# Softmax weights of batches 3 to 7: division in place by GpSimd, halves by one copy and one subtraction

## The chip, the cores and the metric

One core of a Trainium2 chip runs the whole program. The metric is the device time of one execution in microseconds; three runs of the kernel before took 893.05, 891.38 and 894.42 us, a median of 893.05 us. The engines are TensorE (PE, matmuls; its weight loads are listed as PEld), VectorE (DVE), ScalarE (ACT), GpSimd (POOL) and SyncE (SP, whose queue issues the DMAs). Each has its own queue and runs it in order.

## The reference

Windowed attention with a linear bias, then a two-layer MLP with an exact GELU, all in float32:

```python
# q, k, v: (8, 8, 576, 64); w_in: (512, 2048); w_out: (2048, 512)
scores = scale * np.matmul(q, k.transpose(0, 1, 3, 2))
mask = (rel >= 0) & (rel < 128)
scores = np.where(mask, scores + bias[None], -1000000000.0)
scores = scores - np.max(scores, axis=-1, keepdims=True)
attn = np.exp(scores)
attn = attn / (np.sum(attn, axis=-1, keepdims=True) + 1e-09)
x = np.matmul(attn, v)           # then 4608 tokens of 512 values
h = x @ w_in
out = (0.5 * h * (1.0 + erf(h / sqrt(2)))) @ w_out
```

## The kernel before

The 4608 tokens are nine tiles of 512; a batch has 576 tokens, so batch b fills tile b and the first part of tile b+1. While tile t goes through the MLP, batch b = t+1 goes through attention. Float32 accuracy comes from two float16 halves: a value is scaled, its high half is the rounded value, its low half the rest, and a product is three matmuls (high by high, high by low, low by high).

**Attention of one batch** is done in four units, each a pair of heads. A unit has nine groups of 128 rows by 192 keys, in two parts: five groups and four. Its steps: the scores on PE go to five PSUM banks (`scores`, L620); DVE scales them, adds the bias and puts them into the float32 tile `s` (`biased`, L646, five instructions, which is what frees the banks; GpSimd fills masked corners); DVE takes each part's maximum (L729); ScalarE takes the exponentials in place, group by group, with their sums `z` (L733); DVE inverts the sums (L736, L737). The high half of exponential times `z` is written to `e_main`: group by group by ScalarE in batches 1 to 3 (L740), by GpSimd in batches 4 to 7 (L742). The low half is one DVE instruction for each group (`low_part`, L305, called in `low_weights`). Then one DMA for each part transposes `e_main` into the unit's tile `et` (L750). There is one `e_main`, so a part's halves can be written only when the transpose of the same part of the unit before has read it; there are two tiles `s`, taken in turn. PE multiplies `et` by the values for two units at once (`weigh_two`, L846), and the result, again as two halves, is the MLP's input.

**The MLP of a tile**: tiles 2 and 3 go through h = x w_in in 16 blocks (L914) and a GELU each; tiles 4, 5 and 6 go through a form with seven products instead of eight (`Middle`, L1285); the second layer is four blocks of 16 steps (`second`, L961), of which each quarter is 12 matmuls of 512 columns. Tiles 7 and 8 follow with a form of their own.

**The order** is written by hand. `ORDER` (tiles 0 and 1) and `LATER` (tiles 2 to 6) are tables of names, and each name takes one step of a generator; the steps are recorded in that order, so the tables set each engine's queue. In `LATER` the first digit is the tile t, the attention steps being of batch t+1: S0 to S3 are the scores of the four units, B the bias steps, M and N the softmax and low halves (unit, part), Y0 and Y1 the two attention products of units 0 and 1 and of units 2 and 3, X what leaves them, Q and V the loads of the next batch's q, k and v, H and g or the digits 1 to 7 the first layer, o0 to o3 the quarters of the second layer, v and q the statistics and halves of the next batch's values, q and k, K the weights' sums that are stored for the later tiles. `LATER_BANKS` says which of eight PSUM banks each new tile of scores or products takes.

Of the kernel before, what the change touches and what calls it, by code (L numbers as in the profile page):

```python
# [104 lines left out]
2M01 2N01 2M00 2H9 2N00 K K 2H9 2M10 2H10 K 2H10 2N01 2H10 K 2N00 2g9 2N01 2H10 2B2 K 2H11 2g7 2B2 K 2H11 2B2 2g10
2H11 2g8 2B2 2M10 2g9 2N00 2H11 2B2 2g10 2B2 2H12 2g9 2B2 2H12 K 2g11 2B2 2H12 2g10 2B2 2H12 2M20 2H13 K K 2H13 2g12
2H13 2g11 2M10 2H13 2g12 2g11 2H14 K 2g12 2H14 2g13 2M21 2H14 K 2H14 K 2H15 2g14 2g13 2H15 2M10 2g14 2g13 2H15 K 2g14
2H15 K 2o0 2M10 2g15 2M10 2M10 2M10 4gs 2o0 2g15 2M10 2N10 2M10 2g15 2M10 2M10 2N10 2M11 2N10 2N10 2o0 2N10 4gs 2N10
2M11 2M11 2M11 K K 2o0 2M20 K 2M20 2M20 2M11 2M20 2M11 K 2M11 2o1 2M11 2k0 K 2M11 2N11 2M11 2k0 K 2M20 2N11 2M21 K
2N11 2M21 2N11 2Q 2o1 K 2M21 2M21 2M20 2M21 2M20 2M21 2S3 2M20 2N11 2M20 2N20 2M20 2N20 2M20 2o1 2B3 2M20 2N20 2B3 2q  # L110
2B3 2N20 2B3 2B3 2N20 2o1 2Q 2B3 2M30 2B3 2B3 2M30 2M21 2Y0 2B3 2M31 2k1 2M21 2k1 2N21 2M21 2N21 2M21 2M30 2N21 2N21
2M30 2o2 2N20 2M30 2M30 2M31 2M30 2M30 2M31 2M31 2o2 2M31 2N21 2X0 2M31 2M31 2q 2X0 2X0 2o2 2M30 2q 2q 2q 2M30 2q 2N30
2M31 2N30 2M30 2N31 2M31 2N30 2M30 2o2 2M31 2N31 2M30 2N30 2M31 2N31 2X0 2N30 2N31 2N30 2X0 2o3 2X0 2X0 2q 2k2 2X0 2X0
2X0 2q 2q 2X0 2N31 2q 2X0 2o3 2q 2q 2q 2q 2q 2q 2q 2q 2q 2k2 2o3 2q 2q 2Y1 2q K K 2o3 2X1 3U 2X1 K 2X1 K 3H0 K 2X1 3H0
# [1540 lines left out]
```

## Time and profile before

| | us |
|---|---|
| median of three runs | 893.05 |
| the profiled execution | 900.88 |
| its span, first to last instruction | 898.9 |
| PE busy | 856.0 (95%) |
| DVE busy | 733.5 (82%) |
| ACT busy | 612.2 (68%) |
| GpSimd busy | 268.4 (30%) |

The profiled execution took 7.83 us more than the median run, and 1.98 us of it lie outside its span. PE's mean granted clock is 0.988 of full speed. PE is busy for nearly the whole span, but its share is a mean: where it stands still for a few microseconds, it waits for another engine or a DMA, and that place is found in the timeline and not in the share. The attention products of batches 3 to 7 and the tiles 2 to 6 lie between 255.7 and 744.9 us of the span.

### The profile page before, as it was taken

To read this page: it belongs to the slowest core of one execution; us is meant where nothing else is said; L and a number is where in the kernel's file an instruction comes from. 1 tells how busy PE (TensorE), PEld (TensorE's weight loads), DVE (VectorE), ACT (ScalarE), POOL (GpSimd) and SP (SyncE) were. 2 spreads that over 40 slices of the span, in tenths; PEclk is the share of its full clock that TensorE was granted. 3 is DMA by queue.
4 is the path that set the end of the run, shared out by engine and by line. 5 is a ranking of instruction groups with operands and counts; after the bars stand their busy time and mean duration, and the time that the engine had idled before them with its cause. 6 is when DMAs were issued, how large, how long until landed. Compare 5 with 4: busy or idle time off the path is not lost. (4 is left out here: it accounts for less than half of the span.)

```text
span 898.9 us, 21140 instructions
## 1 busy us (share of the span) xinstructions
PE 856.0 (95%) x8580; PEld 523.0 (58%) x8580; DVE 733.5 (82%) x1434; ACT 612.2 (68%) x1236; POOL 268.4 (30%) x445
## 2 busy tenths in 40 slices
PE   6999999999999979899899999999899999999998
PEld 4654444544554445445468645875487544588887
DVE  6999899999779956699967997799887989962871
ACT  7999779895778976494639573874568437642850
POOL 1010000222054802957515446344535420000000
PEclk9999999999999989999989999999999999999999
DMA  9665745562540394326742765276642350031201
GB/s 316 250 202 192 256 115 118 143 164 68 128 118 20 83 243 103 118 53 164 172 165 66 204 127 171 94 212 92 159 151 54 78 118 12 1 106 36 95 1 48
DMA packets 178066, 112.78 MB, mean 125 GB/s; under 512 B 134064, under 2 KB 156720, under 8 KB 175792
## 3 DMA queue, kind: packets, MB, share of 16 engines
q1 hardware_dynamic: 177968, 111.43, 44.7%
q8 instruction: 67, 1.10, 0.5%
q14 instruction: 31, 0.25, 0.1%
HBM read 63.31 MB, written 13.63 MB: 86 GB/s over the span
## 5 line engine op out<-in xcount | busy, mean ns | idle before, releaser
L914 PE MATMUL h<-x,wi 128*128 128x512 f16 x960 | 212.5, 379 | 2.6 <-DVE s L646 1.6
L961 PE MATMUL o<-wo,g 128*128 128x512 f16 x864 | 194.4, 381 | 0.4 <-DVE g L305 0.4
L961 PEld LDWEIGHTS <-g 128*128 128x128 f16 x1152 | 111.0, 98 | 135.5 <-issue 3.2
L914 PEld LDWEIGHTS <-wi 128*128 128x128 f16 x960 | 92.7, 98 | 116.7 <-issue 5.4
L733 ACT ACTIVATE s<-s,nmax 128x192 f32<-128x192 f32 x252 | 111.3, 443 | 57.1 <-DVE nmax L729 56.8
L305 DVE SCALAR_TENSOR_TENSOR e_main<-s,z,e_main 128x192 f16<-128x192 f32 x252 | 114.5, 495 | 21.3 <-ACT e_main L740 11.5
L742 POOL TENSOR_SCALAR e_main<-s,z 128x192 f16<-128x192 f32 x144 | 72.3, 520 | 50.5 <-DVE z L737 28.0
L652 POOL MEMSET s<- 64x128 f32 (+1 forms) x112 | 19.3, 173 | 177.4 <-DVE s L646 153.3
L646 DVE SCALAR_TENSOR_TENSOR s<-sc,cs,bias_h 128x384 f32<-128x384 f32 x112 | 66.9, 606 | 2.6 <-PE sc L620 2.3
L961 PE MATMUL o<-wo_first,g 128*128 128x512 f16 x288 | 66.1, 380 | 1.3 <-DVE e_main L305 1.2
L620 PE MATMUL sc<-kbuf,qbuf 64*64 64x192 f16 (+3 forms) x1656 | 50.4, 252 | 12.8 <-ACT qbuf L521 4.4
L1285 PEld LDWEIGHTS <-t 128*128 128x128 f16 x576 | 56.4, 98 | 7.7 <-issue 1.2
L729 DVE TENSOR_REDUCE nmax<-s 128x5 f32<-128x960 f32 (+1 forms) x56 | 58.1, 1043 | 2.7 <-POOL s L652 2.5
L958 PE MATMUL o<-zo,g 128*128 128x512 f32 x128 | 58.6, 610 | 0.0
L939 POOL TENSOR_SCALAR g<-g,sg 128x512 f16<-128x512 f32 x48 | 41.5, 871 | 55.7 <-ACT g L935 28.4
L740 ACT ACTIVATE e_main<-s,z 128x192 f16<-128x192 f32 x108 | 41.1, 443 | 11.8 <-DMA et<-e_main 8.0
L846 PE MATMUL av<-et,vbuf 64*64 64x64 f16 (+1 forms) x1920 | 32.6, 202 | 17.4 <-DMA et<-e_main 11.6
L733 ACT ACTIVATION_READ_ACCUMULATOR s<-s,nmax 128x1 f32 x252 | 47.2, 187 | 0.0
L305 DVE SCALAR_TENSOR_TENSOR g<-g,sg,g 128x512 f16<-128x512 f32 x48 | 43.3, 921 | 3.9 <-POOL g L939 3.8
L1285 PEld LDWEIGHTS <-wi 128*128 128x128 f16 x432 | 41.9, 98 | 6.4 <-DVE x L305 0.7
L935 ACT ACTIVATE g<-h,gs 128x512 f32<-128x512 f32 x48 | 31.6, 685 | 18.4 <-DVE g L305 12.0
L846 PEld LDWEIGHTS <-vbuf 64*64 64x64 f16 (+1 forms) x1920 | 30.1, 117 | 22.4 <-issue 21.7
(275 smaller groups left out, 1604.2 us busy)
## 6 DMA issues: line engine op xcount, KB each, us to landing
t<-stored SPq DMA_DIRECT2D x12, 1024.0 KB, 5.0
v<-vp SPq DMA_DIRECT2D x32, 320.0 KB, 4.9
out<-ob SPq DMA_DIRECT2D x34, 256.0 KB, 2.2
raw<-w_in SPq DMA_DIRECT2D x8, 1024.0 KB, 10.4
raw<-w_out SPq DMA_DIRECT2D x8, 1024.0 KB, 8.0
q<-qp SPq DMA_DIRECT2D x7, 1152.0 KB, 6.0
k<-kp SPq DMA_DIRECT2D x7, 1152.0 KB, 8.3
stored<-sums SPq DMA_DIRECT2D x8, 512.0 KB, 2.8
```

Of the source, the lines that this page charges most:

```text
L305: return nc.vector.scalar_tensor_tensor(out=dst, in0=src, scalar=scale, in1=high, op0=ALU.mult, op1=ALU.subtract)
L620: done = nc.tensor.matmul(ps[bank][o, n, gap:W], a, m[:, gap:W], start=(i == 0 and (n == 0 or b > 0)), stop=(i == len(terms) - 1 and b > 0 ...
L646: yield nc.vector.scalar_tensor_tensor(out=s[:, bank[0] : bank[0] + k, :], in0=ps[bank][:, 0:k, 0:W], scalar=cs, in1=bias.broadcast_to([P, ...
L729: yield nc.vector.tensor_reduce(out=nmax[:, r], in_=s[:, r], axis=AX.X, op=ALU.max, negate=True)
L733: yield nc.scalar.activation(s[:, i, :], s[:, i, :], AF.Exp, bias=nmax[:, i : i + 1], accum_out=z[:, i : i + 1])
L742: yield nc.gpsimd.tensor_scalar(e[:, i, 0, c], s[:, i], z[:, i : i + 1], 1.0, op0=ALU.mult, op1=ALU.mult)
L846: done = nc.tensor.matmul(o, a, m, start=key not in started, stop=left[key] == 0, skip_group_check=True)
L914: done = nc.tensor.matmul(ph, wi[n][:, a, cc, k * P : (k + 1) * P], x[:, cc, b, :], start=(i == 0), stop=(i == 3 * NCC - 1),)
L939: yield nc.gpsimd.tensor_scalar(g[:, r, 0], g32, gsg[t, n], 1.0, op0=ALU.mult, op1=ALU.mult)
L958: done = nc.tensor.matmul(o, g[:, r, c], zo[n][:, n % 2, k * DM : (k + 1) * DM], start=(fc == first), stop=(fc == last))
L961: done = nc.tensor.matmul(o, g[:, r, a, c], wo[n][:, b, k, :], start=(fc == first and i == 0), stop=(fc == last and i == 2),)
L1285: done = nc.tensor.matmul(ps[:, k * HT : (k + 1) * HT], w(a, i)[:, k * P : (k + 1) * P], m(b, i), start=first and n == 0, stop=True, skip_ ...
```

## The change

A table `HALVES` gives each batch a way to make its halves. Batches 0 to 2 keep theirs (batch 0 has none). In batches 3 to 7 GpSimd multiplies the exponentials by `z` in place, so `s` holds the finished weights in float32; one ScalarE copy for each part then writes the high halves, and one DVE subtraction for each part the low halves. The way "g" of the new code is the old way of batches 4 to 7, and no batch uses it. `LATER`, `LATER_BANKS` and the last entries of `LATER_ROOMS` (which output buffer is taken) are made anew; `ORDER` stays. The lines of `LATER` shown are those around the scores S2 and S3 of batch 5.

```diff
+HALVES = "aaawwwww"
...
 LATER = """
...
-4M10 4M11 4M11 4M11 4M10 4M11 4v 4M10 4v 4v 4v 4M10 4v 4M11 4v 4M11 4S2 4M10 4k0 4M11 4N10 4k0 4M10 4o1 4N11 4M11 4B2
-4M10 4N10 4N11 4M11 4N10 4M10 4N11 4M11 4o1 4N10 4B2 4N11 4N10 4N11 4B2 4v 4B2 4B2 4B2 4o1 4N10 4M20 4B2 4B2 4M20 4v
-4M20 4B2 4v 4M21 4M20 4S3 4M20 4v 4v 4M20 4v 4v 4o1 4v 4B3 4M21 4M21 4M20 4v 4B3 4B3 4M21 4M20 4v 4B3 4M21 4B3 4M20
...
+4M11 4M10 4o0 4M10 4v 4M10 4M11 4M11 4M11 4M11 4S2 4M10 4M11 4M10 4M11 4v 4M10 4v 4v 4v 4o0 4v 4B2 4M10 4M10 4v 4v 4B2
+4B2 4M10 4v 4M10 4v 4v 4B2 4B2 4M10 4M11 4B2 4M11 4S3 4k0 4M11 4M11 4N10 4B2 4M11 4o1 4q 4B2 4N10 4N11 4B2 4M20 4o1 4q
...
@@ -736,17 +733,23 @@
         for i in range(r.start, r.stop):
-            if st.b < 4:
+            if HALVES[st.b] == "a":
                 yield nc.scalar.activation(e[:, i, 0, c], s[:, i], AF.Copy, scale=z[:, i : i + 1])
                 continue
-            yield nc.gpsimd.tensor_scalar(e[:, i, 0, c], s[:, i], z[:, i : i + 1], 1.0, op0=ALU.mult, op1=ALU.mult)
+            to = e[:, i, 0, c] if HALVES[st.b] == "g" else s[:, i]
+            yield nc.gpsimd.tensor_scalar(to, s[:, i], z[:, i : i + 1], 1.0, op0=ALU.mult, op1=ALU.mult)
+        if HALVES[st.b] == "w":
+            yield nc.scalar.copy(e[:, r, 0, c], s[:, r])
 
     def low_weights(st, part):
 
         r, c, banks = RANGES[part]
         e = e_main
-        for i in range(r.start, r.stop):
-            yield low_part(e[:, i, 1, c], st.s[:, i], st.z[:, i : i + 1], e[:, i, 0, c])
+        if HALVES[st.b] == "w":
+            yield nc.vector.tensor_tensor(out=e[:, r, 1, c], in0=st.s[:, r], in1=e[:, r, 0, c], op=ALU.subtract)
+        else:
+            for i in range(r.start, r.stop):
+                yield low_part(e[:, i, 1, c], st.s[:, i], st.z[:, i : i + 1], e[:, i, 0, c])
```

SP's queue in tile 2, batch 3, of the kernel before: `et3_1` is the transposed tile of unit 1, `q32_4` and `k32_4` are the loads for batch 4, `stored` the stores of the weights' sums.

```order
L750 DMA_TRANSPOSE et3_1_3857<-e_main_95 128x20x128
L1069 DMA stored1_104<-sums1_0_3738 128x2048
L975 DMA out_0<-ob2_0_3903 128x512
L527 DMA q32_4_3918<-qp 128x4x576
L1069 DMA stored1_104<-sums1_1_3865 128x2048
L750 DMA_TRANSPOSE et3_1_3857<-e_main_95 128x16x128
L527 DMA k32_4_4043<-kp 128x4x576
L975 DMA out_0<-ob2_1_4251 128x512
L750 DMA_TRANSPOSE et3_2_4276<-e_main_95 128x20x128
L750 DMA_TRANSPOSE et3_2_4276<-e_main_95 128x16x128
L750 DMA_TRANSPOSE et3_3_4355<-e_main_95 128x20x128
L750 DMA_TRANSPOSE et3_3_4355<-e_main_95 128x16x128
```

The same place of SP's queue in the changed kernel.

```order
L753 DMA_TRANSPOSE et3_1_3840<-e_main_95 128x20x128
L1072 DMA stored1_104<-sums1_0_3689 128x2048
L753 DMA_TRANSPOSE et3_1_3840<-e_main_95 128x16x128
L524 DMA q32_4_3992<-qp 128x4x576
L978 DMA out_0<-ob2_0_3904 128x512
L1072 DMA stored1_104<-sums1_1_3845 128x2048
L753 DMA_TRANSPOSE et3_2_4265<-e_main_95 128x20x128
L753 DMA_TRANSPOSE et3_2_4265<-e_main_95 128x16x128
L524 DMA k32_4_4300<-kp 128x4x576
L753 DMA_TRANSPOSE et3_3_4321<-e_main_95 128x20x128
L753 DMA_TRANSPOSE et3_3_4321<-e_main_95 128x16x128
```

The second transpose of unit 1 moved ahead of the load of q, and the load of k moved from ahead of unit 2's transposes to between those of units 2 and 3.

DVE's queue in batch 5 of the kernel before, from the first bias step of unit 2 (`s5_2`) on; the rows of `e_main` are the low halves of unit 1.

```order
L646 SCALAR_TENSOR_TENSOR s5_2_6901<-sc5_2_0_6820,cs5_5789,bias_h_64 128x384
L305 SCALAR_TENSOR_TENSOR e_main_95<-s5_1_6735,z5_1_6766,e_main_95 128x192 x7
L646 SCALAR_TENSOR_TENSOR s5_2_6901<-sc5_2_2_6821,cs5_5789,bias_h_64 128x384
L280 TENSOR_REDUCE top_6930<-turned_6817 32x1
L646 SCALAR_TENSOR_TENSOR s5_2_6901<-sc5_2_4_6822,cs5_5789,bias_p_65 128x192
```

The same place in the changed kernel, to the last bias step of unit 2.

```order
L643 SCALAR_TENSOR_TENSOR s5_2_6832<-sc5_2_4_6750,cs5_5808,bias_p_65 128x192
L643 SCALAR_TENSOR_TENSOR s5_2_6832<-sc5_2_5_6751,cs5_5808,bias_h_64 128x384
L977 TENSOR_SCALAR ob4_0_6914<-o4_0_6681,so4_4729 128x512
L749 TENSOR_TENSOR e_main_95<-s5_1_6660,e_main_95 128x5x192
L643 SCALAR_TENSOR_TENSOR s5_2_6832<-sc5_2_7_6752,cs5_5808,bias_h_64 128x384
L749 TENSOR_TENSOR e_main_95<-s5_1_6660,e_main_95 128x4x192
```

Before, seven low halves of unit 1 stood between the first and the second bias step of unit 2; now the two subtractions of unit 1 stand behind the fourth and the fifth.

ScalarE's queue in batch 6 of the changed kernel, with the copies (`e_main`) among the exponentials of the next unit and the halves of the next q and k.

```order
L742 CAST e_main_95<-s6_1_8209 128x5x192
L730 ACTIVATE s6_2_8330,z6_2_8453<-s6_2_8330,nmax6_2_8438 128x192 x4
L742 CAST e_main_95<-s6_1_8209 128x4x192
L730 ACTIVATE s6_2_8330,z6_2_8453<-s6_2_8330,nmax6_2_8438 128x192 x5
L534 ACTIVATE qbuf_91,stq7_8499<-q32_7_8308 128x2304
L534 ACTIVATE kbuf_92,stq7_8499<-k32_7_8314 128x2304
L742 CAST e_main_95<-s6_2_8330 128x5x192
```

Before, there was nothing of `e_main` on ScalarE in batches 4 to 7; each copy now stands in its queue until GpSimd has divided the part, and the exponentials behind it with it.

## Rows read from the trace of the kernel before

**Rows 1.** Busy time by engine in stages: tiles 2 to 6, one row each.
```profile
255.70:358.00 102.30, 94.72 (x933) 47.20 (x932) 78.92 (x153) 82.43 (x160) 41.55 (x56) 0.97 0.47 114
358.00:464.20 106.20, 97.61 (x985) 48.49 (x984) 86.55 (x167) 61.05 (x123) 67.62 (x97) 0.97 0.51 136
464.20:558.50 94.30, 90.76 (x1183) 61.78 (x1181) 78.64 (x173) 64.48 (x131) 45.94 (x74) 1.00 0.52 139
558.50:652.50 94.00, 88.31 (x1075) 59.93 (x1076) 82.02 (x175) 59.87 (x125) 41.88 (x74) 1.00 0.55 139
652.50:744.90 92.40, 90.80 (x1136) 61.51 (x1135) 79.36 (x151) 51.73 (x122) 36.26 (x68) 1.00 0.38 94
```

**Rows 2.** PE in order of time: start, length, work, idle before and what ended it.
```profile
318.65 5.35 PE L961 MATMUL o<-wo,g 128*128 128x512 f16 x24
...
330.34 3.99 PE L846 MATMUL av<-et,vbuf 64*64 64x64 f16 x154 [5.90 <-DMA et<-e_main]
...
366.12 0.71 PE L620 MATMUL sc<-kbuf,qbuf 64*64 64x192 f16 x25 [2.12 <-DVE x L305]
...
428.42 0.71 PE L620 MATMUL sc<-kbuf,qbuf 64*64 64x192 f16 x25 [0.64 <-DVE x L305]
...
451.50 3.99 PE L846 MATMUL av<-et,vbuf 64*64 64x64 f16 x154 [3.69 <-DMA et<-e_main]
...
513.97 1.28 PE L620 MATMUL sc<-kbuf,qbuf 64*64 64x192 f16 x54
...
621.12 2.78 PE L846 MATMUL av<-et,vbuf 64*64 64x64 f16 x192
...
741.97 0.22 PE L846 MATMUL av<-et,vbuf 128*64 128x64 f16 x3 [1.28 <-issue]
```

**Rows 3.** What PE waited for in the attention products: us in total, times, longest.
```profile
PE av L846 <- DMA et<-e_main: 11.6, 3, 5.9
PE av L846 <- issue: 5.8, 4, 1.7
```

**Rows 4.** Stretches of low granted clock, PE's busy time first, PEclk third from last.
```profile
327.80:334.60 6.80, 4.26 (x155) 3.92 (x155) 1.86 (x6) 6.17 (x20) 0.00 (x0) 0.50 0.96 278
450.70:457.50 6.80, 6.00 (x159) 4.52 (x159) 1.10 (x3) 2.30 (x2) 1.81 (x1) 0.50 0.70 218
```

**Rows 5.** SP's queue in order of time, around the load of q.
```profile
318.86 0.38 SPq L527 DMA_DIRECT2D q<-qp  x1
...
320.72 7.49 SPq L750 DMA_TRANSPOSE et<-e_main  x1
```

**Rows 6.** Transposes: landing of the one at 320.72, then all by the page.
```profile
DMA to landing us min/median/max: 9.6/9.6/9.6
...
et<-e_main SPq DMA_TRANSPOSE x56, 4.2
```

**Rows 7.** Groups of instructions by form: count, busy us, mean ns, idle before.
```profile
L305 DVE SCALAR_TENSOR_TENSOR e_main<-s,z,e_main 128x192 f16<-128x192 f32 x252 | 114.5, 495 | 21.3 <-ACT e_main L740 11.5 <-POOL e_main L742 9.3
L742 POOL TENSOR_SCALAR e_main<-s,z 128x192 f16<-128x192 f32 x144 | 72.3, 520 | 50.5 <-DVE z L737 28.0 <-DMA et<-e_main 8.1 <-ACT s L733 7.5
L740 ACT ACTIVATE e_main<-s,z 128x192 f16<-128x192 f32 x108 | 41.1, 443 | 11.8 <-DMA et<-e_main 8.0 <-ACT s L733 1.8 <-DVE z L737 1.7
L1068 DVE TENSOR_TENSOR sums<-sums 128x1024 f16<-128x1024 f32 x8 | 11.9, 1494 | 10.1 <-ACT sums L1067 10.1
L1105 DVE TENSOR_TENSOR xs<-xr,xs 128x1024 f16<-128x1024 f32 x3 | 3.7, 1220 | 0.1
L1067 ACT CAST sums<-sums 128x1024 f16<-128x1024 f32 x8 | 8.3, 1039 | 16.4 <-POOL sums L1065 16.4
```

**Rows 8.** DVE in order of time: third bias steps, batches 4 and 5, and low halves.
```profile
377.22 0.41 DVE L646 SCALAR_TENSOR_TENSOR s<-sc,cs,bias_p 128x192 f32<-128x192 f32 x1
...
516.95 2.93 DVE L305 SCALAR_TENSOR_TENSOR e_main<-s,z,e_main 128x192 f16<-128x192 f32 x7
...
520.43 0.40 DVE L646 SCALAR_TENSOR_TENSOR s<-sc,cs,bias_p 128x192 f32<-128x192 f32 x1
```

More of the change, by code (lines that the diff above doesn't have):

```diff
@@ L105 @@
[L105 to L114, printed above, removed]
@@ new lines @@
+K 2g2 2H5 K 2H5 2g4 2v 2v 2v 2v 2v 2v 2S1 2g3 2M00 2v 2v 2v 2v 2g4 2g3 2H5 K 2H5 2M00 2B1 2M00 2g4 2H6 2B1 2g5 2B1 2H6
+2M00 2v 2H6 2B1 2B1 2B1 2H6 2M00 2M01 2M10 2B1 2M00 2H7 2M00 2H7 2M00 2B1 2M00 2H7 2v 2M01 2v 2M00 2v 2v 2M01 2v 2g5
+2H7 2v 2v 2M01 2v 2B1 2H8 2g5 2M00 2H8 2M01 2M11 2g6 2H8 2M01 2N00 2M01 2H8 2H9 2g7 2N00 2M01 2H9 2g8 2M01 2H9 2M01 K
+2g6 2H9 2M01 2H10 2H10 2M10 2N01 2S2 2g7 2g6 2M10 2N01 2H10 2M10 2g8 2H10 2B2 2g9 2H11 2g7 K 2H11 2g8 2H11 2g10 2B2
+2H11 2g9 2M10 2B2 2H12 2g10 2g9 2H12 2B2 K 2H12 2B2 2g11 2B2 2H12 2g10 2B2 K 2H13 2B2 2H13 2g12 2M20 2g11 2H13 2M10
@@ new lines @@
+2g12 2g11 2H13 K 2H14 2g12 2g13 2H14 K 2M10 2H14 2M10 K 2H14 2M11 2M10 2H15 2g13 2H15 2M10 2g13 2H15 2M10 2g14 2H15
+2M10 2M10 2o0 2B2 2M21 2g15 2g14 2M10 4gs 2g15 2g14 2M11 2o0 2g15 2N10 2M11 2M11 4gs 2N10 K K 2o0 2M20 2M20 2M20 2M11
+2M20 2o0 2M20 2M21 2M11 K 2M20 2M21 2M21 2M20 2M11 2M21 2M11 2M21 2M11 2M21 2o1 2k0 2M11 K 2M11 K 2N11 2M20 2S3 2N11
+2M20 2M20 2o1 2B3 2M20 2M20 2B3 2B3 2Q 2M20 K 2k0 2B3 2B3 2M21 2N20 2M21 2o1 2B3 2M21 2M30 2M21 K 2M21 2B3 2B3 2o1 K
+2B3 2M30 2M30 2M30 2N21 2M30 2Y0 2k1 2M31 2M30 2q 2M30 2M30 2M30 2M30 2o2 2M30 2N20 2M30 2M31 2M30 2M31 2M31 2M31 2o2
@@ new lines @@
+2X0 2N21 2M31 2M31 2M31 2X0 2M31 2X0 2X0 2M31 2X0 2X0 2X0 2M31 2Q 2M30 2X0 2o2 2X0 2X0 2N30 2M31 2X0 2N30 2X0 2N31 2o2
+2o3 2q 2k2 2N31 2k1 2q 2q 2o3 2k2 2q 2q 2q 2q 2q 2q 2q 2q 2q 2q 2q 2q 2q 2q 2q 2o3 2q 2q 2Y1 2q K 2o3 2X1 3U 2X1 2X1
+3H0 K 2X1 3H0 2k3 2X1 2X1 3H0 2X1 K 2k3 2X1 3H0 K 2X1 2X1 3H1 2X1 3g0 K 2X1 3U 3H1 K 3H1 3H1 3S0 3g1 4gs 3V 3H2 3B0
+3g0 3V K 3H2 3B0 3g1 3H2 3H2 3B0 3H3 3g2 3V 3g0 3B0 3H3 K 3V 3B0 3H3 3B0 3H3 3M00 3B0 3g2 3S1 3g3 K 3B0 3M00 3g1 3H4
+3B0 3g3 3H4 3B1 3M00 3H4 3M01 K 3M00 3H4 3B1 3M00 3B1 K 3H5 3M00 3g2 3B1 3g4 K 3H5 3B1 3B1 3H5 K 3M00 3H5 3g3 3B1 3M01
@@ new lines @@
+3g4 3H6 3B1 3M00 3H6 3M10 3B1 3M00 3H6 3M00 3g5 3M00 3g4 3H6 3M00 3M11 3H7 3M00 3H7 3v 3g6 3g5 3H7 3M00 3g6 3H7 3M01
+3H8 3H8 3N00 3H8 3M01 3H8 3M01 3g5 3N00 3g7 3H9 3M01 3g6 3H9 3M01 3v 3v 3v 3M01 3v 3H9 3v 3v 3M01 3v 3g8 3v 3H9 3M01
+3v 3v 3M10 3v 3M01 3v 3H10 3v 3g7 3v 3v 3v 3H10 3v 3v 3g8 3v 3H10 3g7 3M01 3H10 3g8 3M10 3H11 3M10 3N01 3M10 3H11 3M10
+3N01 3H11 3M11 3M10 3M10 3H11 3M11 3M10 3M11 3M10 3H12 3M11 3M10 3H12 3M10 3g9 3M11 3M11 3M10 3H12 3M11 3M11 3H12 3M11
+3H13 3g10 3M11 3g9 3g11 3H13 3g10 3M10 3g9 3H13 3g11 3H13 3M11 3g10 3H14 3g12 3H14 3g11 3g13 3g12 3H14 3N10 K 3g13
@@ new lines @@
+3H14 3H15 3g14 3H15 3N11 3S2 3N10 3g14 3g12 3H15 K 3H15 3g13 3o0 3g15 3N11 K 3g14 3g15 3o0 3B2 5gs K 3g15 3B2 K 3B2
+5gs K 3o0 3B2 3B2 K 3B2 3M20 K K 3o0 3M20 3M20 3B2 3B2 3M20 K 3S3 3M20 3k0 3M20 3B2 3k0 K 3B3 3Q 3M21 3Y0 3B3 K 3B3
+3M21 K 3M20 3M21 3M20 3B3 3B3 3M21 3M20 3B3 3M21 3M20 3o1 3M30 3M20 3X0 3M20 3M20 3M21 3X0 3M30 K 3M21 3X0 3M20 3M21
+3M21 3o1 K 3M21 3M30 3M30 3M30 3N20 3M30 3o1 3M21 3X0 3M30 3N20 3X0 3B3 3M21 3B3 3M30 3X0 3B3 3q 3M30 3N21 3M30 3o1
+3M31 3M30 3N21 3M30 3M31 3M30 3M31 3Z0 3M31 3o2 3Q 3M31 3M30 3M31 3M31 3X0 3N30 3M31 3o2 3X0 3N30 3M31 3X0 3X0 3M31
@@ new lines @@
+3X0 3X0 3M31 3Z0 3M31 3o2 3Z0 3N31 3Z0 3q 3N31 3Z0 3o2 3q 3q 3q 3q 3q 3q 3q 3q 3q 3q 3q 3q 3q 3o3 3q 3q 3q 3q 3k2 3k2
+3k1 3Y1 3q 3q 3k1 3o3 4T1 3X1 3q 3Z0 4U 3Z0 3o3 3X1 4T0 3X1 3X1 3X1 3X1 3X1 3Z1 3o3 3X1 3X1 3X1 3Z1 3X1 3X1 3Z1 4S0
+3k3 3Z1 3k3 410 4B0 3Z1 4B0 4B0 3Z1 420 4B0 4a0 3Z1 411 4a0 421 4U 4a1 4a0 460 461 4c0 4a0 4a1 4T2 4B0 4a1 4B0 450 4c1
+4a0 4a1 4M00 470 4B0 4B0 4M00 451 4a1 4B0 4M01 471 4d0 5gs 4M00 4d0 4M00 440 4d1 4M00 4d1 4M00 430 4T3 4e0 4M00 4M00
+4M00 4M00 441 4c0 4M00 4M00 4c0 4e0 431 4e1 4c0 4e0 4d0 4e1 412 4d1 4c1 4M01 4d0 4c0 422 4d1 4d0 4M00 4a2 413 4M01 4a2
@@ new lines @@
+4B3 4N11 4M21 4B3 4B3 4M20 4o1 4v 4v 4k0 4q 4B3 4B3 4M20 4B3 4M20 4M30 4M20 4B3 4M20 4M21 4M20 4B3 4M21 4o1 4M20 4v
+4B3 4M21 4q 4q 4M20 4M31 4M21 4M20 4M30 4M20 4M21 4q 4M21 4M20 4M30 4v 4q 4v 4v 4q 4M20 4v 4M30 4q 4v 4q 4v 4M21 4M20
+4q 4Y0 6gs 4q 4M21 6gs 4q 4q 4M21 4q 4M30 4N20 4M21 4M30 4M31 4M30 4M31 4q 4M30 4q 4o2 4q 4M30 4N20 4M21 4M30 4M30
+4M31 4N21 4M30 4M31 4X0 4M31 4M31 4k1 4M30 4X0 4o2 4X0 4M31 4N21 4X0 4q 4M31 4X0 4X0 4M31 4M31 4Z0 4k1 4o2 4M30 4X0
+4N30 4Z0 4M31 4X0 4N30 4N31 4o2 4Z0 4X0 4X0 4q 4q 4Z0 4N31 4o3 4q 4Z0 4o3 4k2 5T0 4Z0 4X0 4k2 4X0 4Y1 4Z0 4o3 4X1 5T1
@@ new lines @@
+5M30 5M30 5v 5q 5v 5q 5B3 5B3 5M21 5v 5q 5B3 5v 5q 5M30 5M31 5o1 5N20 5X0 5N21 5M31 5M31 5M30 5v 5M31 5M30 5v 5X0 5M30
+5v 5M31 5X0 5M30 5v 5o2 5q 5X0 5v 5N21 5v 5M31 5M30 5v 5k1 5M31 5v 5X0 5M30 5X0 5X0 5q 5M30 5v 5q 6v 5M31 5q 5X0 5M31
+5M30 5X0 5M31 5q 5o2 6v 5q 5M31 5q 5X0 5N30 5Z0 5M31 5q 5N30 5o2 5N31 5Z0 5q 5X0 5N31 5q 5q 5q 5X0 5Z0 5o2 5Z0 5k1 5Z0
+5q 5q 5o3 5q 5Z0 5Y1 5Z0 5k2 6T0 5o3 5X1 6T1 6U 5X1 5k2 5X1 5o3 5X1 5X1 5X1 5X1 5Z1 5X1 5o3 5X1 5X1 5Z1 5X1 5X1 5Z1
+5Z1 5Z1 610 6U 5Z1 5k3 6S0 6a0 5k3 620 6B0 6T2 5Z1 6B0 611 6a0 6B0 621 6a1 6B0 6B0 6a0 6B0 660 6a1 6B0 6B0 661 6M00
@@ L178 @@
 )
 LATER_ROOMS = (
-    "0120120120120120120120120120120120120120120120120120120120120120"
+    "0120120120120120120120120120120120120120120120120120121021021021"
 )
```

93 lines of the change are left out of this document (30 added, 63 removed).

## The prediction

> **What bounds the kernel now.** I read the busy time by stage first, since the whole span mixes in stages that the change doesn't touch. In the five stages of tiles 2 to 6 PE is busy for 88.3 to 97.6 us of 92.4 to 106.2 [rows 1]; it idles there for 7.58 + 8.59 + 3.54 + 5.69 + 1.60 = 27.0 us. DVE comes next with 78.6 to 86.6 us busy; ScalarE has 20 to 45 us free in a stage and GpSimd 39 to 61. PE's own work doesn't change, so the change can give back no more than these 27.0 us and what they cost in clock.
>
> Then PE in order of time, to see where the idle time lies [rows 2], and its waits in sum [rows 3]. The attention products stand out: seven waits inside them, 11.6 us put down to the transpose and 5.8 to nothing ("issue"). Each lies between matmuls that read one part of `et` and matmuls that read the next, so I take all seven, 17.4 us, as waits for a transpose. The longest are 5.90 us at 330.34 (batch 3, first product) and 3.69 at 451.50 (batch 4, second product); the other five, 7.8 us, are in batches 5 to 7. The two long ones have a second price: around each lies a stretch of 6.80 us at half the granted clock, the lower of its two levels, with 4.26 and 6.00 us of PE work in it [rows 4]. At the upper level that work takes half as long, so 2.13 and 3.00 us are lost.
>
> Last, SP in order of time before the longest wait. The load of the next q is issued at 318.86 and the transpose that PE waits for at 320.72; it holds SP for 7.49 us [rows 5] and lands 9.6 us after its issue, where the median of 56 is 4.2 [rows 6].
>
> **The change part by part.** *Work of the engines.* DVE loses 20 units of 9 low halves, 180 x 0.495 = 89.1 us [rows 7], and gains 40 subtractions, 20 of 960 columns and 20 of 768. The nearest rows subtract 1024 columns of the same types in 1.220 and in 1.494 us [rows 7]; by columns that is 1.14 to 1.40 and 0.92 to 1.12, 41 to 50 us in all. DVE saves 39 to 48 us, some 8.7 a stage. ScalarE gains 40 copies, at most 0.97 and 0.78 us by the 1.039 of 1024 columns, 35 us, and loses batch 3's 36 scalings of 0.443, 15.9 us [rows 7]. GpSimd gains batch 3's 36 divisions, 18.7 us at 0.520; the other 144 now write float32, for which I take the same 0.520. All of it fits into the free time of [rows 1], and I count nothing for it. If ScalarE's cover fails, a copy costs its 0.97 us and the wait for GpSimd, up to five divisions or 2.6 us, in which the next unit's exponentials, or the copies that free the first layer's banks, are queued behind it.
>
> What the subtraction costs beside GpSimd is where the skill speaks against the change. The two rows differ by 0.27 us. The Trainium skill, SBUF — State Buffer, section "SBUF: two separate sides", says that a DVE instruction with two SBUF inputs and a GpSimd instruction that reads SBUF shut each other out for the whole instruction, whichever starts second standing still. By that rule a subtraction could lose a whole division, 0.52 us, so 40 of them 21 us, and a division could stand for 1.1 to 1.4 us behind a subtraction. DVE would still save 18 to 27 us; the old low halves too have two SBUF inputs.
>
> *The chain of a unit.* Before: last division, last low half (0.495), transpose. Now: last division, copy (0.97), subtraction (1.1 to 1.4), transpose; a part on its own ends 1.6 to 1.9 us later. Against that, a division no longer writes `e_main` and needn't wait until the transpose of the unit before has read it; behind a late transpose the chain is now 2.1 to 2.4 us and was 5 x 0.52 + 0.495 = 3.1. I take 1.7 us later, the case without that wait.
>
> *Term A, batch 3's first product.* The second transpose of unit 1 now stands ahead of the load of q in SP's queue. Issued at 318.86 and landing after 4.2 us it would be there at 323.1, before PE reaches the product (its wait began at 324.4). So 5.90 + 2.13 = 8.0 us can go. The copy of this part stands behind unit 2's exponentials, so I take 7.5; the other end is 0.
>
> *Term B, batch 4's second product.* What covers PE between the scores S3 and the second product is counted in quarters of the second layer, 2.67 us each (24 matmuls took 5.35), and the first product, 2.78 [rows 2]. By the tables batch 4 had 7 quarters there, 18.7 us, and now has 9 and the first product, 26.8. Its scores ended at 429.1 and `et` was there at 451.5, 22.4 us later [rows 2]; with 1.7 more that is 24.1, inside the cover. But the load of k is now issued between the transposes of units 2 and 3, in batch 3 too, and a transpose behind a load landed 9.6 - 4.2 = 5.4 us late. Then `et` is there after 29.5: a wait of 2.7 us, and a slow clock of up to 3.0. So B is 6.7 us at best and 1.0 at worst; I take 5, nearer to the best, as only the first of the two transposes is issued close behind the load.
>
> *Term C, batches 5 to 7.* Their waits sum to 7.8 us. The quarters between S3 and the second product go from 7 to 10, 11 and 8, so the cover grows by 8.0, 10.7 and 2.7 us; batch 7's wait of 1.28 and the 1.7 of the longer chain are 0.3 more than its 2.7. I take 6.5; the other end is 0.
>
> *Term D, scores that come early.* The price of the cover is that scores follow each other closely, and the later ones take banks that DVE's bias steps must have read. In batch 5, S3 now comes one quarter (2.67 us) behind S2, no longer four, and takes three of its banks. S2 ended at 515.25 [rows 2] and its third bias step at 520.83 [rows 8], 5.6 us later. As late as that, S3 waits 2.9 us; S1 of batch 4 and S3 of batch 6 (5.3 us of cover) 0.3 each, and S2 of batch 6 (4.0) 1.6: 5.1 together. Batch 4's S0 had its third bias step 10.8 us behind it (366.8 to 377.6, [rows 2, 8]), which makes S1's wait 5.5 and the sum 10.3. Of the 5.6 us, 2.93 were seven low halves of unit 1 [rows 8], which now stand behind the fourth bias step as subtractions; without them nothing waits. I charge 3, between 0 and 10.3.
>
> *Term E, the rest of the order.* 27.0 - 17.4 = 9.6 us of the five stages' idle time are small waits for banks and DVE. A new order has its own, and I can't follow each. The bounds are 9.6 us either way; I charge 6.
>
> The sum is -7.5 - 5 - 6.5 + 3 + 6 = -10 us: 900.88 becomes 890.9 in a profiled execution, and the median 893.05 becomes 883. The profiled execution is 7.83 us above the median, so some waits may be shorter without the profiler; the range allows for that.
>
> **The rivals.** *The waits only move (no change).* For it: the load of k goes to where it can meet the last transposes of batches 3 and 4. Against it: the cover there is 10 quarters and the first product in batch 3, 29.5 us, and 26.8 in batch 4. If A's 7.5 is met by the like at batch 3's second product, B gives 1, C 6.5, and D and E cost 9, the sum is +1.5: 894.5.
>
> *Early scores wait for DVE (slower).* Place: S1 of batch 4, S3 of batch 5, S2 and S3 of batch 6, S3 of batch 7, with covers of 5.3, 2.7, 4.0, 5.3 and 8.0 us. The price is the lateness of the third bias step less these. At 9 us they wait 3.7 + 6.3 + 5.0 + 3.7 + 1.0 = 19.7; with A to C kept at 19 and E at 6 that is +6.7: 900. It decides from a lateness of some 8 us (2.7 + 5.3 + 4.0 + 2.7 = 14.7 against 13). For it: the 10.8 in batch 4. Against it: DVE has 8.7 us less to do in each stage, and half of batch 5's lateness was low halves.
>
> *More than forecast.* All of A to C (22.5), D and E at nothing: 870.5.
>
> *The change doesn't do what it says*: subtractions stand beside GpSimd and DVE saves little. By the rows it saves at least 39 us, and DVE's free time stays above 12 us in each stage even if it saves nothing, so what it costs is D's sum at full lateness, 5.1 for 3: 885, within the forecast.
>
> **How the numbers follow.** The forecast, a gain of 3 to 16 us: 0.57. More than that: 0.08. The waits only move: 0.18. Slower: 0.17. About 0.3%, 2.7 us, is what a measurement of this kernel can tell from no change. So faster is 0.65, same 0.18, slower 0.17. The predicted time is 883. The forecast's own range is 877 to 890; the one for 8 in 10 goes from 874 to 897, over the case of no change into the near part of the slower one.
>
> **What would show it.** Right: no wait at batch 3's first product and no half clock there; less than 1 us of waiting in each second product of batches 4 to 7; 40 subtractions of 0.9 to 1.4 us in place of 180 low halves; 14 to 20 us of PE idle in the five stages for 27.0. Wrong: scores that wait more than 2 us each for bias steps in batches 4 to 6; a wait of 4 us or more, with half the clock, at batch 3's or 4's second product behind the load of k; a copy on ScalarE waiting for GpSimd while PE waits for a bank of the first layer.

## The result, and the profile after

The changed kernel takes 881.02 us (median of 4, 877.79 to 883.64) where the kernel before took 893.33 beside it (891.38 to 894.42): a ratio of 0.9863, 95% interval 0.9826 to 0.99, 12.3 us less. Its profiled execution took 883.64 us with a span of 881.8.

The one profiled execution of before that the prediction works with, 900.88 us, stood 8 us above its median. I therefore set after against a second one, of 892.11 us (first experiment). First the busy time by stage, tiles 2 to 6 from row to row (columns as in [rows 1]), of before in that second execution:

```profile
252.50:352.10 99.60, 94.31 (x933) 46.93 (x932) 79.08 (x153) 82.27 (x160) 42.50 (x56) 0.98 0.45 117
352.10:456.00 103.90, 96.23 (x985) 47.94 (x984) 85.90 (x166) 61.17 (x123) 66.67 (x96) 0.98 0.51 135
456.00:550.70 94.70, 90.77 (x1183) 61.80 (x1181) 79.27 (x175) 64.47 (x131) 45.88 (x74) 1.00 0.53 144
550.70:644.00 93.30, 88.29 (x1075) 59.95 (x1075) 81.83 (x174) 59.88 (x125) 41.90 (x74) 1.00 0.55 141
644.00:736.10 92.10, 90.63 (x1136) 61.52 (x1135) 79.56 (x152) 51.73 (x122) 36.05 (x68) 1.00 0.38 95
sum 483.60, PE 460.23 PEld 278.14 DVE 405.63 ACT 319.53 POOL 232.99; mean PE 92.05 PEld 55.63 DVE 81.13 ACT 63.91 POOL 46.60
```

and of after:

```profile
255.20:351.60 96.40, 94.27 (x932) 46.02 (x931) 67.50 (x125) 74.39 (x132) 55.51 (x90) 0.98 0.52 121
351.60:452.80 101.20, 96.36 (x1040) 47.83 (x1039) 81.06 (x146) 70.49 (x133) 68.40 (x98) 1.00 0.50 136
452.80:547.20 94.40, 90.81 (x1130) 61.46 (x1128) 73.84 (x146) 65.30 (x133) 43.71 (x74) 0.98 0.54 146
547.20:637.90 90.70, 88.33 (x1078) 59.68 (x1076) 79.09 (x151) 68.11 (x135) 45.73 (x74) 1.00 0.53 151
637.90:727.00 89.10, 89.10 (x1130) 60.69 (x1129) 76.43 (x125) 56.89 (x130) 36.57 (x68) 1.00 0.38 92
sum 471.80, PE 458.86 PEld 275.67 DVE 377.92 ACT 335.19 POOL 249.92; mean PE 91.77 PEld 55.13 DVE 75.58 ACT 67.04 POOL 49.98
```

The five stages are 11.8 us shorter, which is nearly the 12.3 of the medians, and 10.4 of it is idle time of PE: 483.60 - 460.23 = 23.4 us before, 471.80 - 458.86 = 12.9 after. The two whole executions differ by less, 8.5 us: ahead of the stages, where no step was changed, after took 2.7 us longer (255.2 for 252.5), with two stretches at the lower clock for one, and behind them 0.8 longer. What PE waited for in them (total, times, longest), before in its second execution:

```profile
PE av L846 <- DMA et<-e_main: 8.9, 3, 3.7
PE av L846 <- issue: 5.1, 4, 1.4
PE sc L620 <- DVE x L305: 3.1, 3, 1.3
...
PE o L961 <- DVE e_main L305: 1.1, 1, 1.1
```

and after, the rows that answer to [rows 3]:

```profile
PE h L917 <- ACT g L938: 2.1, 1, 2.1
PE av L849 <- issue: 4.5, 3, 2.2
PE av L849 <- DMA et<-e_main: 1.8, 1, 1.8
PE av L849 <- DVE s L643: 1.6, 2, 1.3
...
PE sc L617 <- DVE s L643: 0.3, 1, 0.3
```

Waits for a transpose fell from 8.9 to 1.8 us: that is 7.1 of the 10.4. "issue" inside the products hardly moved (it is no wait for a transpose, as the last experiments show). Scores wait 0.3 us for bias steps. The half clock costs nearly the same in both executions: in the five stages two stretches of 3.41 us each,

```profile
324.75:328.16 3.41, 3.33 (x138) 3.27 (x139) 1.53 (x4) 3.29 (x12) 0.00 (x0) 0.50 1.01 377
444.22:447.63 3.41, 2.94 (x123) 2.88 (x123) 0.18 (x1) 0.00 (x0) 1.50 (x1) 0.50 0.76 223
```

before, at the end of the long waits in batch 3's first and batch 4's second product, and after

```profile
275.65:279.06 3.41, 3.41 (x10) 1.21 (x9) 3.35 (x8) 3.37 (x9) 1.63 (x4) 0.50 0.00 0
538.50:541.90 3.40, 3.26 (x38) 1.81 (x38) 0.61 (x2) 2.48 (x2) 0.00 (x0) 0.50 0.63 188
```

each at the end of a wait of over 2 us or just behind it (in tile 2's first layer and in batch 5's second product).

### The profile page after: what moved, and what is told of

Same layout as the page of the kernel before. It is cut to its first block, busy times and chain, and to the rows that moved or that the text cites. A ratio compares the mean times of both kernels' runs of the same rounds, so it can differ in the third digit from the quotient of the medians.

```text
span 881.8 us, 21037 instructions
## 1 busy us (share of the span) xinstructions
PE 853.3 (97%) x8580; PEld 520.5 (59%) x8580; DVE 699.9 (79%) x1294; ACT 626.0 (71%) x1234; POOL 285.8 (32%) x481
## 4 chain that ended last, share of the span: by engine, by line
PE 51%; DVE 23%; ACT 12%; DMA 7%; issue 4%; POOL 4%; SPq 0%; ACTq 0%; DVEq 0%; POOLq 0%
PE o L964 14%; PE u L1288 7%; PE h L917 6%; PE v L1288 5%; PE u_out L1390 4%; DVE g L302 3%; ACT s L730 3%; DVE s L643 3%; PE u L1186 2%; PE av L849 2%; PE sc L617 2%; DVE nmax L726 2%; DMA raw<-w_out 2%; PE v L1186 2%; DVE e_main L302 2%
## 5 line engine op out<-in xcount | busy, mean ns | idle before, releaser
L740 POOL TENSOR_SCALAR s<-s,z 128x192 f32<-128x192 f32 x180 | 89.5, 514 | 53.1 <-DVE z L734 40.5
L942 POOL TENSOR_SCALAR g<-g,sg 128x512 f16<-128x512 f32 x48 | 41.4, 869 | 52.2 <-DMA q<-qp 26.7
L742 ACT CAST e_main<-s 128x960 f16<-128x960 f32 (+1 forms) x40 | 36.3, 909 | 29.0 <-POOL s L740 22.5
L749 DVE TENSOR_TENSOR e_main<-s,e_main 128x960 f16<-128x960 f32 (+1 forms) x40 | 44.8, 1119 | 11.6 <-ACT e_main L742 11.4
L961 PEld LDWEIGHTS o<-zo,g 128*128 128x128 f32 x128 | 24.4, 194 | 28.2 <-issue 25.9
L617 PEld LDWEIGHTS <-qbuf 64*64 64x64 f16 x1512 | 30.4, 107 | 16.9 <-issue 15.9
```

What stands on the lines that cost most here:

```text
L617: done = nc.tensor.matmul(ps[bank][o, n, gap:W], a, m[:, gap:W], start=(i == 0 and (n == 0 or b > 0)), stop=(i == len(terms) - 1 and b > 0 ...
L740: yield nc.gpsimd.tensor_scalar(to, s[:, i], z[:, i : i + 1], 1.0, op0=ALU.mult, op1=ALU.mult)
L749: yield nc.vector.tensor_tensor(out=e[:, r, 1, c], in0=st.s[:, r], in1=e[:, r, 0, c], op=ALU.subtract)
L942: yield nc.gpsimd.tensor_scalar(g[:, r, 0], g32, gsg[t, n], 1.0, op0=ALU.mult, op1=ALU.mult)
L961: done = nc.tensor.matmul(o, g[:, r, c], zo[n][:, n % 2, k * DM : (k + 1) * DM], start=(fc == first), stop=(fc == last))
```

## The experiments

**The kernel before once more.**

> The kernel before, unchanged, for a second profiled execution. Theory (the wait of 5.9 us at batch 3's first product and the half clock behind it belong to the one profiled execution of before and not to its usual runs, as its 900.88 us stand 8 us above the median): 889 to 895 us, under 3 us of wait at that product, no half clock there, and the five stages of tiles 2 to 6 in 479 to 483 us for 489.2. Rival (the wait is usual, and its time is found elsewhere in other runs): 5 us or more there again.

892.11 us, clock 0.994. The wait at batch 3's first product was there, but 3.67 us long, with one stretch of 3.41 us at the lower level behind it; the first profile had 5.90 and 6.83. So each theory was half right: wait and half clock came in both executions, and a good 2 us of the one and half of the other in the first alone. The stages took 483.6 us, just above the range.

**New halves and new order apart.** Two kernels take one without the other.

```diff
 # new_halves_old_order: HALVES, softmax and low_weights of after; LATER, LATER_BANKS, LATER_ROOMS of before
-2M10 2N11                  (last step of a part; its last low half)
+2M10 2M10 2N11             (one more for the copy; the subtraction where the last low half stood)
 # old_halves_new_order: LATER, LATER_BANKS, LATER_ROOMS of after
-HALVES = "aaawwwww"
+HALVES = "aaaagggg"
```

> The new halves with the old order and its banks: each copy stands right behind the last division of its part, each subtraction where the part's last low half stood. Theory (the order brings the gain): 893 us (889 to 899). The wait of 5.9 us at batch 3's first product and the one of 3.7 us at batch 4's second product stay, each with its half clock; the second products of batches 5 to 7 wait up to 1.7 us longer each, and the small waits for DVE give back some 4 us. Rival (the new halves bring the gain by DVE's relief): 884 us or less.

> The new order and its banks with the old halves: HALVES is aaaagggg, each division and each low half stands where the new order has the divisions and the subtraction, and the copies are gone. DVE has 180 low halves of 0.495 us, 89 us, for 40 subtractions, 44.8 us: some 9 us more in each of the five stages; a part ends some 1.7 us earlier for want of the copy. Theory (the order brings the gain, and it is the relief of DVE that lets scores follow each other closely): half of the gain is lost, 888 us (884 to 895), with 2 to 6 us more of waiting of scores and products for DVE's bias steps. Rival 1 (the order alone brings it): 881 us, within 2.5. Rival 2 (the new halves bring it): 893 us or more.

> The new order with the old halves once more, HALVES aaaagggg, but each division of the next unit is held back until the transpose of the same part of the unit before has been recorded; in the first version five such divisions stood ahead of it and wrote over halves that had not been read. Theory (DVE's low halves make the chain of a unit too long for closely spaced scores): 896 us (892 to 900), with 25 to 32 us from the end of the scores S3 to the last low half in batches 4 to 6, for 22 to 29 with the new halves. Rival (only the divisions out of place made the first version slow): 885 us or less.

| | us | ratio to before (95%) |
|---|---|---|
| new halves, old order | 915.01 | 1.0244 (1.0219 to 1.0268) |
| old halves, new order | 897.90 | 1.0053 (1.0034 to 1.0073) |
| the same, divisions held back | 893.88 | 1.0015 (0.9998 to 1.0032) |

The first version with the old halves leaves out an order that these need: three divisions in batch 3 and two in batch 5 write over halves of unit 2 before its transpose has read them. Only the held one is used below. My theory missed the first kernel by 22 us: the new halves in the old order, which was not made anew for them, are slower by 2.4%. DVE's relief is there, 371.4 us busy in the five stages for 405.6, and is worth nothing: PE's idle time there is 38.1 us for 23.4, and with six stretches of half clock, 30.7 us in all for 6.8, its work takes 9.1 us longer. With the old halves the new order gains nothing: my theory of half the gain and the first rival's 881 fall, and the second rival's 893 or more stands. The held kernel's 893.88 lies in its range, its chain in batch 6 (33.9 us, below) does not. Where the time went (PE's waits, new halves in the old order; then old halves in the new order, held):

```profile
PE av L848 <- DMA et<-e_main: 17.0, 4, 6.5
PE h L916 <- DVE s L642: 5.1, 1, 5.1
```

```profile
PE av L852 <- DMA et<-e_main: 13.4, 3, 6.7
PE av L852 <- DVE s L646: 4.7, 2, 4.4
```

Both wait for transposes, for opposite reasons. Two times decide, both from the end of a batch's last scores, S3: the chain, to the end of its last low half or subtraction, and the cover, until PE comes to the second product (after, batch 5: 503.8 to 528.2 and to 534.1 us). Chain / cover, from the timelines:

| us | batch 4 | 5 | 6 | 7 |
|---|---|---|---|---|
| before | 16.4 / 18.2 | 17.4 / 22.6 | 20.9 / 22.3 | 14.9 / 22.7 |
| new halves, old order | 18.9 / 18.1 | 22.9 / 23.7 | 24.0 / 24.0 | 17.8 / 26.9 |
| old halves, new order, held | 28.9 / 34.2 | 27.5 / 29.9 | 33.9 / 31.3 | 20.1 / 23.5 |
| after | 22.3 / 29.2 | 24.4 / 30.3 | 28.7 / 31.3 | 17.5 / 23.6 |
| after with more reductions | 26.0 / 32.1 | 26.0 / 30.3 | 33.4 / 31.3 | 20.8 / 23.6 |

In the ten cases in which the cover is at most 2.8 us longer than the chain, the product waits for a transpose, 0.55 to 6.48 us; in the ten in which it is 3.4 or more longer, it doesn't. In the old order the new halves lengthen the chain by 2.5 to 5.5 us, and its cover, made for the shorter one, doesn't reach. In the new order, where scores follow each other closely, DVE has several units' bias steps and halves in its queue; there the new halves shorten the chain by 2.6 to 6.6 us. Only together do cover and chain fit.

**DVE's relief taken back.**

```diff
-            yield nc.vector.tensor_tensor(out=e[:, r, 1, c], in0=st.s[:, r], in1=e[:, r, 0, c], op=ALU.subtract)
+            done = nc.vector.tensor_tensor(out=e[:, r, 1, c], in0=st.s[:, r], in1=e[:, r, 0, c], op=ALU.subtract)
+            nc.vector.tensor_reduce(out=st.nmax[:, r], in_=st.s[:, r], axis=AX.X, op=ALU.max, negate=True)
+            yield done
```

> The changed kernel with one more DVE reduction of the finished weights behind each of the 40 subtractions, into the maxima that nobody reads any more: some 1.04 us each, 42 us in the five stages, which is DVE's relief taken back, and it lies off the chain of its own unit. Theory (DVE's relief pays, as scores and halves queue on it): 887 us (884 to 891). Rival (DVE's free time was worth nothing, only the order and the shape of the chain count): 881 us, within 2.5.

886.29 us, ratio 0.9922 (0.9902 to 0.9943): 5.3 us more than after, as the theory had it. The rival's 881 falls, if narrowly: the intervals of the two ratios just don't meet (0.9902 and 0.9900). The reductions lie off their own unit's chain, and yet the chains grow by 1.6 to 4.7 us (last line of the table), and PE waits

```profile
PE av L851 <- DMA et<-e_main: 6.1, 2, 5.6
PE av L851 <- DVE s L643: 3.8, 2, 3.5
```

5.6 us of it at batch 6's second product, whose chain grew most, and 3.5 at batch 4's first, whose bank waits for a late bias step.

**Batch 3's transpose alone.**

```diff
-2N11 2Q 2o1 K 2M21 2M21 2M20 2M21 2M20 2M21 2S3 2M20 2N11 2M20
+2N11 2o1 K 2M21 2M21 2M20 2M21 2M20 2M21 2S3 2M20 2N11 2Q 2M20
```

> The kernel before, with one edit: in batch 3 the load of the next q stands behind the second transpose of unit 1 on SP and no longer ahead of it. Theory (the load ahead of it made that transpose late, and the wait with its half clock can simply go): 885.5 us (883 to 888), no wait over 0.5 us at batch 3's first product and no half clock there. Rival (the wait moves to a later product or to scores): 893 us, with a new wait of 4 to 8 us within the next 60 us.

891.92 us, ratio 0.9989 (0.9971 to 1.0006): the rival was right. In order of time on PE:

```profile
319.66 0.50 PE L845 MATMUL av<-et,vbuf 64*64 64x64 f16 x38
320.95 2.46 PE L845 MATMUL av<-et,vbuf 64*64 64x64 f16 x154 [0.80 <-DMA et<-e_main]
...
341.58 0.50 PE L845 MATMUL av<-et,vbuf 64*64 64x64 f16 x38
346.20 3.81 PE L845 MATMUL av<-et,vbuf 64*64 64x64 f16 x154 [4.12 <-DMA et<-e_main]
```

The first product's wait is gone (0.80), and 20 us later the second one waits 4.12. Unit 3's last low half ended 25.7 us behind S3, when PE was nearly at the product (27.2 behind); its transpose landed at 346.16. In after, where ScalarE no longer scales batch 3's groups, that chain takes 21.1 us, and the product comes 28.7 us behind S3. With the old halves in the same order (held) it takes 31.3, and the product waits 6.72.

**The waits that nothing explains.** Two edits set out to remove waits of after: the second product of batches 5 and 6 a quarter later, and then, besides, a statistic in tile 2 later.

```diff
-4Y1 4Z0 4o3 4X1
+4Z0 4o3 4Y1 4X1
-5Y1 5Z0 5k2 6T0 5o3 5X1
+5Z0 5k2 6T0 5o3 5Y1 5X1
-2H2 2v 2H3 ... 2H5 2g4 2v 2v 2v 2v 2v 2v 2S1
+2H2 2H3 ... 2H5 2g4 2v 2v 2v 2v 2v 2v 2v 2S1
```

> The changed kernel with the second attention product of batches 5 and 6 one quarter of the second layer later. Theory (the waits of 2.24 us with its half clock and of 1.76 us there are those for late transposes, and one more quarter of 2.67 us covers them): 878.5 us (876 to 880), no wait over 0.5 us in these two products, and up to 1.3 us more at the start of the next tile's first layer, which needs what leaves the product. Rival (the next tile's first layer waits instead for what leaves the product): 881 us or more.

> The kernel with the second products of batches 5 and 6 a quarter later, and besides the first step of the statistics of batch 4's values, one DVE reduction that stood 4.4 us waiting for its load, behind the maximum and the low halves of the GELU that were queued behind it. Theory: the first-layer wait of 2.13 us and its half clock (1.7 us) in tile 2 go as well, 875.5 us (873 to 878). Rival (its half clock and wait are not usual, or scores wait instead): 878 us, the same as without this edit.

879.56 us, 0.9859 (0.9836 to 0.9882), and 875.89, 0.9822 (0.9799 to 0.9845). The second edit did what it should: the reduction had kept DVE from the low halves of the GELU while its load was on its way, and without it tile 2's wait, 1.39 us with the first edit alone, is gone (its half clock was gone already). The first did not, though 879.56 lies in its range: its ratio is that of after, 0.9863. Batch 6's wait for a transpose went, but a wait of 1.38 and 1.06 us put down to "issue" came in its place, and batch 5's second product waits 3.57 and 2.99 us where after waits 2.24. Of the second kernel, PE and SP in order of time:

```profile
529.47 2.08 PE L848 MATMUL av<-et,vbuf 64*64 64x64 f16 x148
534.54 0.89 PE L848 MATMUL av<-et,vbuf 128*64 128x64 f16 x44 [2.99 <-issue]
```

```profile
519.15 4.26 SPq L752 DMA_TRANSPOSE et<-e_main  x2
526.55 0.33 SPq L1078 DMA_DIRECT2D t<-stored  x1
```

The transposes had landed at 525.43. DMA from 531.60 to 532.25, and from there to 533.40 (queue: packets, MB, share; q1 carries the loads and stores, q8 instructions):

```profile
q1 hardware_dynamic: 89, 0.15, 60.3%
```

```profile
q8 instruction: 1, 0.02, 5.2%
q1 hardware_dynamic: 1, 0.00, 0.0%
```

While the rest of the 1024 KB of `t` came in, no instruction packet moved; it ran from 532.30 to 533.26, and PE went on 1.28 us later. This is PE's own program: on the whole span of after the page has

```profile
q8 instruction: 67, 1.10, 0.5%
```

for PE's 8580 matmuls and 8580 weight loads, which is 256 of them to a packet. In after, the three "issue" waits in the products end at 442.91, 517.98 and 538.64, and a packet of PE's instruction queue ended 1.2 to 1.6 us before each (441.53, 516.78, 537.03). Two kernels put that to the test: a load taken away from the product, and then another product moved to where a load runs.

```diff
-5T0 4Z0 4X0 4k2 4X0 4Z0 4o3 4Y1 4X1 5T1 5U
+4Z0 4X0 4k2 4X0 4Z0 4o3 4Y1 4X1 5T1 5T0 5U
 # quarter_ahead_of_product, besides
-3Q 3M21 3Y0 3B3
+3Q 3M21 3o1 3Y0 3B3
 # (and the quarter's old place, a little further on, is gone; the banks are renamed)
```

> The kernel with the second products of batches 5 and 6 a quarter later and the statistics later, and one more edit: the load of the first stored sums of tile 5, 1024 KB, is issued behind the second one, which waits for batch 5's second product, and no longer 3 us ahead of that product. In the kernel without this edit the transposes of that product had landed at 525.4 and PE still stood still in it from 531.56 to 534.54, while PE's own program, 16 KB on its instruction queue, was loaded from 532.30 to 533.26, just behind the 1024 KB, which landed at 531.92. Theory (PE waits there for its program, and the program waits behind the 1024 KB): the wait falls from 2.99 us to 1.0 to 1.4 and the half clock behind it goes, 873 us (871 to 875), less up to 1 us if the first layer then waits for the sums. Rival (the wait is one for data that the product reads, whatever else is loaded): 3 us of wait stay, 876 us.

> The same with one more edit: in batch 4 one quarter of the second layer stands ahead of the first attention product instead of behind it, and takes the bank that the product took first (the later banks are renamed alike). Theory (the product stood 2.1 us in all waiting for banks that the scores S2 and S3 just ahead of it hold until DVE's bias steps): 1 to 1.5 us less than without this edit. Rival (the product meets a bank of S3 instead, or its place in PE's program now meets a program load): no difference, within 1 us.

873.43 us, 0.9782 (0.9757 to 0.9807), the fastest of all, and 877.72, 0.9836 (0.9812 to 0.9859). With the load behind the product:

```profile
528.57 2.08 PE L848 MATMUL av<-et,vbuf 64*64 64x64 f16 x148
530.93 0.89 PE L848 MATMUL av<-et,vbuf 128*64 128x64 f16 x44 [0.28 <-issue]
```

```profile
518.93 4.26 SPq L752 DMA_TRANSPOSE et<-e_main  x2
526.95 0.34 SPq L977 DMA_DIRECT2D out<-ob  x1
531.85 1.67 SPq L1078 DMA_DIRECT2D t<-stored  x2
```

the instruction packet ran from 528.55 to 529.51 and the wait is 0.28 for 2.99, less than the theory's 1.0 to 1.4: the packet starts with the product's first matmul, where it had started 2.8 us behind it. The rival's 3 us of waiting for data fall. In the last kernel batch 4's first product waits 1.02 us for a bank, and then

```profile
407.49 2.57 PE L848 MATMUL av<-et,vbuf 64*64 64x64 f16 x176 [1.02 <-DVE s L642]
414.07 0.48 PE L848 MATMUL av<-et,vbuf 128*64 128x64 f16 x10 [4.01 <-issue]
```

```profile
407.00 0.38 SPq L523 DMA_DIRECT2D q<-qp  x1
```

4.01 us: the 1152 KB of q, issued at 407.00, landed at 412.26, and the instruction packet ran from 411.72 to 412.68. A stretch of 6.83 us at half clock follows, with 5.99 us of PE work in it. The rival had named a program load there, but not its price: 4.3 us slower than without the edit.

## Why the prediction was right, and where its steps failed

The size came out right (883 forecast, 881.02 measured) by terms that were off both ways, so its closeness is luck. Against the second execution of before, PE's idle time by place:

| term | forecast | measured | |
|---|---|---|---|
| A, batch 3's first product | -7.5 | -3.7 | wait all gone; its size was that of one execution |
| B, batch 4's second product | -5 | -2.8 | 3.67 for a transpose gone, 0.88 for a program load there |
| C, products of batches 5 to 7 | -6.5 | -1.3 | 1.37 + 1.43 + 1.60 + 1.32 + 0.98 = 6.7 before, 1.36 + 2.24 + 1.76 = 5.4 after |
| D + E, early scores and the rest | +9 | -2.6 | other idle time 9.3 before, 6.7 after |

That is the 10.4 of idle time; the other 1.4 of the 11.8 lie in PE's busy time. The forecasts of A and B hold a slow clock too, 2.13 us in A. With half of the PE work in the two stretches of before, 1.67 and 1.47 us, A comes to -5.3 and B to -4.3; but two stretches came elsewhere, with 3.41 and 3.26 us of work, so the half clock gave nothing in all. By the signs that I had set, batch 3's first product is as forecast, the idle time fell further (12.9 us for 14 to 20), and the second products of batches 5 and 6 failed: 2.24 and 1.76 us for less than 1.

*A.* The step held in place. The second transpose of unit 1 is issued ahead of the load of q:

```profile
317.41 2.95 SPq L753 DMA_TRANSPOSE et<-e_main  x1
320.53 0.46 SPq L524 DMA_DIRECT2D q<-qp  x1
```

for 320.72 and 7.49 us in [rows 5], and the product has no wait. What I added to it unsaid is that the time, once gained, is kept. Alone it is not, as the fourth experiment shows; in the new order the new halves' shorter chain in batch 3 keeps it (21.1 us, for 31.3 and a wait of 6.72 with the old halves).

*B.* Right, for the reason given. The product stands 29.2 us behind S3 (410.7 to 439.9) and the last subtraction ends at 433.0. With the new halves in the old order, where it stands 18.1 us behind, it waits 6.48.

*C* failed in "I take all seven, 17.4 us, as waits for a transpose". The 5.8 us put down to "issue" in [rows 3] are loads of PE's program: in that trace a packet of 16 KB on q8 ended 1.25 to 1.39 us before the end of each of the four waits. A quarter more of cover did not shorten batch 5's (3.57 us for 2.24). And the chain of batches 4 to 7, forecast 1.7 us longer, became 2.6 to 7.8 longer, 7.0 in batch 5 and 7.8 in batch 6: the cover that I counted, 8.0 and 10.7, was mostly used up by the longer chain that the closer scores bring.

*D* was right in size and wrong in place. Scores waited 0.3 us; the price, 2.05 us, is paid by batch 4's first product, which stands right behind S3 and needs banks of S2 and S3 (1.31 and 0.31) and of an output (0.43). The rival of early scores that wait for DVE came out in no kernel here. Nearest to it are the old halves in this order: there too the scores hardly wait, but batch 4's first product waits 4.39 us for a bias step.

*E* was charged at +6 for want of knowledge; the other waits did not grow.

*The engines' work.* By form, copy, subtraction and the low halves that stay, after:

```profile
L742 ACT CAST e_main<-s 128x960 f16<-128x960 f32 x20 | 19.7, 987 | 18.3 <-POOL s L740 14.1 <-DMA et<-e_main 4.2
L749 DVE TENSOR_TENSOR e_main<-s,e_main 128x960 f16<-128x960 f32 x20 | 24.9, 1245 | 8.5 <-ACT e_main L742 8.5
L302 DVE SCALAR_TENSOR_TENSOR e_main<-s,z,e_main 128x192 f16<-128x192 f32 x72 | 26.6, 410 | 4.8 <-ACT e_main L737 4.6
L749 DVE TENSOR_TENSOR e_main<-s,e_main 128x768 f16<-128x768 f32 x20 | 19.9, 994 | 3.1 <-ACT e_main L742 2.9
```

1.245 and 0.994 us lie inside the forecast ranges, and the copy's 0.987 just above the 0.97 that I had called its most. The prediction took 0.495 us for a low half, the mean of all 252 in [rows 7]. But the 72 of batches 1 and 2, which stay, take 0.410 (third line), so the 180 that went took 252 x 0.495 - 72 x 0.410 = 95.2 us and not 89.1. The subtractions take 44.8: 50.4 saved in operations, above the 39 to 48, but 33.6 by the page's busy time (733.5 to 699.9). Neighbouring instructions overlap there: the 252 add up to 124.7 us and are busy for 114.5. What stands beside GpSimd shows in the divisions (shortest, median and longest):

```profile
L740 POOL TENSOR_SCALAR s<-s,z x180: 417/425/2371, 279.5 to 709.2; 128x192 f32<-128x192 f32 x180
L749 DVE TENSOR_TENSOR e_main<-s,e_main x40: 935/1138/2103, 284.0 to 711.9; 128x960 f16<-128x960 f32 x20, 128x768 f16<-128x768 f32 x20
```

The 12 divisions that ran into a subtraction took 1.12 to 2.37 us, the median one 0.425. The rule of the Trainium skill, SBUF — State Buffer, section "SBUF: two separate sides", that the second of the two stands still, agrees with that. But mostly it was GpSimd that stood, and it had the time; the subtractions lost some 3.4 us in all (44.8 against 20 x 1.13 + 20 x 0.94 = 41.4), not the up to 21 that I weighed.

## What to carry to other kernels

Cheaper work and a closer order can each be worthless alone: price a change of one by the chain from the last scores to the product that needs them, in the order in which it will run, and set it against the cover. Before a wait in a profile becomes a term, ask in a second execution how long it is, and what the next wait on the same path will be once it is gone. And where "issue" stands in a stretch of very many small instructions, look at the instruction queue and keep large loads away from it.
